# Attention inputs of a fused kernel loaded as one packed array, with a new order of work

## The chip, the cores and the metric

The kernel runs on one core of a Trainium2 chip. The metric is device time of one execution in microseconds (us), lower is better. A core has a matmul engine (PE, with its weight loads shown apart as PEld), three engines for elementwise work (DVE, ACT, POOL), and SP, which here only issues DMA loads and stores. Each engine takes its own instructions strictly in order. They wait for each other through semaphores.

## The reference

Sliding-window attention, then a mixture of experts with soft slots, then a gated feed-forward layer. All is f32.

```python
def _attn_ref(q, k, v):                      # 4 batches, 8 heads, 576 tokens, 64 wide
    scores = scale * np.matmul(q, k.transpose(0, 1, 3, 2))
    # heads 0-3: the last 32 tokens; heads 4-7: every 4th of the last 128
    scores = np.where(masks[None, :, :, :], scores, -1000000000.0)
    scores = scores - np.max(scores, axis=-1, keepdims=True)
    attn = np.exp(scores)
    attn = attn / (np.sum(attn, axis=-1, keepdims=True) + 1e-09)
    return np.matmul(attn, v).astype(np.float32)

def _moe_ref(x, phi, w1, w2):                # x: 2304 x 512
    logits = x @ phi                         # 8 experts x 4 slots
    d = softmax of logits over tokens;  slot_input = d.T @ x
    slot_out[e] = np.maximum(slot_input[e] @ w1[e], 0.0) @ w2[e]
    c = softmax of logits over slots;   return c @ slot_out

def _moe2_ref(x, w_in, w_out):               # 512 -> 2048 -> 512
    h = x @ w_in
    g = h * (1.0 / (1.0 + np.exp(-h)))
    return g @ w_out
```

## The kernel before

**Stages.** Two heads of one batch make a pair; there are 16 pairs. Stage one (0 to 97.4 us in the profile) is attention over the pairs together with the softmaxes of the slots, a batch after every fourth pair. Stage two (97.4 to 129.1 us) passes the slots through the experts: 16 pieces of w1 (operations `L1.0` to `L1.15`), then 16 of w2 (`L2.0` to `L2.15`, the last in two halves). Stage three folds the slots' output into w_in, and then runs the feed-forward layer over 6 groups of 384 tokens until the end. Its 864 large matmuls (`om`) are the bulk of the time: of each unit of hidden values, `si` (ACT, line 794) makes the plain value, `gh` (ACT at first, line 799) a rounded one and `gl` (DVE) the rest. Stage three can't begin before the last piece of w2 has been multiplied.

**One pair n, by the names of the operations.** `lq`, `lk`, `lv` load q, k and v, 288 KB each, 2304 bytes a partition (lines 165 to 184). `qx`, `qy` spread q into a padded place (POOL, line 180). `vx`, `vy` write a masked copy of v (line 197 on POOL, 199 on ACT, 201 on DVE). `M` and `S` put mask and scores into PSUM (PE, 36 matmuls for `S`). `rm` is the row maximum (DVE, 227), `ex` nine exponentials (ACT, 232), `rc` the reciprocal sums (DVE, 244), `nm` the normalization (POOL, 249), `pt` four transposes (DVE, 256 to 263). `pv` multiplies with v (PE, in two parts, `.0` and `.1`), `xe` copies the result out of PSUM (ACT, 299 or 301), `T` transposes it (PE, line 312), `te` copies that (ACT, 315), `lt` makes the logits (PE). For each batch `da`, `dt`, `dm`, `db`, `dq`, `dr`, `dsub`, `dex`, `dc` carry the softmax over tokens, and `caa` to `cag` the one over slots.

**What sets the order.** `op(name, engine, cost, deps, fn)` records each operation. `list_schedule` (line 1049) then plans all of them: it places an operation on its engine when its inputs are ready by the planner's own costs, and where several are ready the one with the longest path to the end plus a bonus by kind from the table `PRIO` goes first. The program is emitted in that order, so the table decides what stands behind what on every engine. The loads are chained by hand instead: the string `ATT` (line 1022) gives the order of SP's queue, `q` for the next pair's q and k, `v` for the next v, `w` for the next piece of w1 or w2. SP issues in that order, and a load whose place is still in use holds back all loads behind it.

**Places.** k, q and v have separate rings: k five places, then three, q four, v four, then two (`kslot`, `qslot`, `rslot`, lines 110 to 117), spread over the buffers `k`, `raw`, `more0` and `more1`. `more0` and `more1` become w15 and w16 when attention is done with them.

Of the kernel before, what the change touches and what calls it, by code (L numbers as in the profile page):

```python
# [32 lines left out]
def fused_kernel(ctx: ExitStack, tc: tile.TileContext, a: dict):  # L33
# [12 lines left out]
    dm = hsb[0:1, 352:352 + 5 * NS]  # L46
# [32 lines left out]
    def reg(key, off, n):  # L79
        return tiles[key][:, off:off + n]  # L80
# [25 lines left out]
    for place, key in (("ra", "a0"), ("rb", "a1"), ("rk", "k"), ("rv", "v"), ("rs", "raw"), ("rt", "px"), ("x", "xb"), ("w15", "more0"), ("w16", "more1")):  # L106
        new(place, key)


    def kslot(n):  # L110
        return n % 5 if n < 10 else (n - 10) % 3

    def qslot(n):
        return n % 4

    def rslot(n):
        return n % 4 if n < 12 else n % 2

    def before(slot, n):
        return max((m for m in range(n) if slot(m) == slot(n)), default=None)  # L120

    def kreg(n):
        i = kslot(n)
        return reg("k", 608 * i, 608) if i < 3 else reg(f"more{i - 3}", 1152, 608)

    def qraw(n):
        i = qslot(n)
        return reg("raw", 576 * i, 576) if i < 2 else reg("more0", 576 * (i - 2), 576)

    def vraw(n):  # L130
        if n == NPAIR - 1:
            return vz
        i = rslot(n)
        return reg("raw", 1152 + 576 * i, 576) if i < 2 else reg("more1", 576 * (i - 2), 576)

# [46 lines left out]
    def load_v(n):  # L182
        b, p = divmod(n, 4)
        sp.dma_start(out=vraw(n), in_=a["v"][b, p])

# [3 lines left out]
    def veng(n):  # L189
        return VY[n % 4] if n > 1 else "DVE"  # L190
# [141 lines left out]
    for n in range(NPAIR):  # L332
        b, p = divmod(n, 4)
        kb, rb = before(kslot, n), before(rslot, n)
        qb, vb = before(qslot, n), rb if n < NPAIR - 1 else None
        op(f"lk{n}", "SP", .74, [f"S{kb}"] if kb is not None else [], lambda n=n: load_k(n))
        op(f"lq{n}", "SP", .74, [f"qx{qb}", f"qy{qb}"] if qb is not None else [], lambda n=n: load_q(n))
        op(f"lv{n}", "SP", .74, [f"vx{vb}", f"vy{vb}"] if vb is not None else [], lambda n=n: load_v(n))
        for z in range(2):
            op(f"q{'xy'[z]}{n}", "DVE" if z and n not in QP else "POOL", .7, [f"lq{n}", f"S{n-2}" if n >= 2 else None], lambda n=n, z=z: spread(n, z))  # L340
        for z in range(2):
            op(f"v{'xy'[z]}{n}", veng(n) if z else "POOL", {"POOL": 1.4, "ACT": .68, "DVE": .745}[veng(n) if z else "POOL"], [f"lv{n}", f"pv{n-2}.1" if n >= 2 else "izm", ("nm0", "rc0")[z] if n == 1 else None], lambda n=n, z=z: vmask(n, z))
# [3 lines left out]
        op(f"S{n}", "PE", 1.11, [f"M{n}" if n else "fl0", f"lk{n}", f"qx{n}", f"qy{n}", f"iq{n}" if n < 5 else None] + [f"iz{c}{n}" for c in "ab" if n < 2] + free,  # L346
           lambda n=n: scores(n))
# [215 lines left out]
    att_r = [f"{c}{n}" for c in ("qx", "qy") for n in (N1 - 3, N1 - 2)] + [f"{c}{n}" for c in ("vx", "vy") for n in (N1 - 2, N1 - 1)]  # L563
    att_v = [f"pv{N1}.1", f"S{N1}"]
    free2 = {"rs": att_r, "ra": [f"pv{N1-1}.1", f"S{N1-1}"], "rk": [f"S{N1}"], "rb": att_v, "rv": att_v, "rt": att_v + [f"T{N1}", f"lt{N1}"],
             "w15": ["qx14", "qy14", "qx15", "qy15", "S8"], "w16": ["vx10", "vy10", "vx11", "vy11", "S9"]}
    for i in range(16):
# [345 lines left out]

    for n in range(5):
        op(f"iq{n}", "DVE", .1, [], lambda n=n: iq(n))
# [245 lines left out]
def lay(inputs):  # L1161
# [12 lines left out]
    out = {}  # L1174
    out["q"] = np.ascontiguousarray(heads(inputs["q"]).transpose(0, 1, 2, 4, 3)).reshape(B, 4, 128, S)
    out["k"] = np.ascontiguousarray(heads(inputs["k"]).transpose(0, 1, 2, 4, 3)).reshape(B, 4, 128, S)
    v = heads(inputs["v"]).reshape(B, 4, 2, NJ, 2, 32, D)
    out["v"] = np.ascontiguousarray(v.transpose(0, 1, 4, 2, 5, 3, 6)).reshape(B, 4, 128, NJ * D)
    row = np.arange(128)
# [38 lines left out]
```

## Time and profile before

| what | us |
|---|---|
| median of 3 runs | 360.08 (359.61 to 360.41) |
| the profiled execution | 360.57 |
| span from its first to its last instruction | 358.4 |
| PE busy in stage one, 0 to 97.4 | 90.81 |
| PE busy in stage two, 97.4 to 129.1 | 31.68 of 31.70 |
| PE busy in stage three, 129.1 to 358.4 | 224.17 of 229.30 |

The span is what the trace covers; the rest of the execution's 360.57 us lies around it. "Busy" is the time in which an engine has at least one instruction under way; where it is not busy, the trace names what ended the wait. Rates are given in GB/s of all loads together.

### The profile page before, as it was taken

What the parts mean: (1) busy time and instruction counts of PE and PEld (TensorE: products, weight loads), DVE (VectorE), ACT (ScalarE), POOL (GpSimd) and SP (SyncE); (2) the same over time, 40 slices, a digit from 0 to 9 for tenths busy, and PEclk for the clock granted to TensorE, in tenths of its full rate; (3) what the DMA queues carried; (4) which work ended last, traced back from release to release, by engine and by line L of the source; (5) the groups of instructions that cost most, each with busy time, mean ns of one, the idle gap of its engine ahead of it and who ended that gap; (6) DMA issues with size and microseconds to landing.
All of it is one profiled execution on the core that took longest, in us unless ns stands there. A gap on an engine that the chain in (4) does not pass through costs nothing.

```text
span 358.4 us, 7976 instructions
## 1 busy us (share of the span) xinstructions
PE 346.7 (97%) x3118; PEld 263.2 (73%) x3118; DVE 236.9 (66%) x547; ACT 165.1 (46%) x558; POOL 74.5 (21%) x121
## 2 busy tenths in 40 slices
PE   7999999998999989999999999999999999999995
PEld 3686877776533347877888888787888888888884
DVE  5877778699620589999999764585444744474445
ACT  3698989786240146594433342546522222222220
POOL 6988978565420000000000000000000000000000
PEclk9999999999999999999999999999999999999999
DMA  7999999999999999462630000000000400040004
GB/s 255 404 408 404 406 396 409 405 417 414 419 400 422 408 423 416 165 234 92 261 117 0 2 0 0 3 0 3 0 0 2 176 0 2 0 176 2 0 0 176
DMA packets 17460, 70.02 MB, mean 195 GB/s; under 512 B 1936, under 2 KB 2448, under 8 KB 11664
## 3 DMA queue, kind: packets, MB, share of 16 engines
q1 hardware_dynamic: 17424, 69.53, 49.2%
q8 instruction: 24, 0.39, 0.4%
q14 instruction: 12, 0.10, 0.1%
HBM read 64.80 MB, written 4.72 MB: 194 GB/s over the span
## 4 chain that ended last, share of the span: by engine, by line
PE 90%; ACT 3%; DVE 2%; POOL 1%; issue 1%; DMA 1%; DVEq 0%; ACTq 0%; POOLq 0%
PE ps L86 86%; PE ps L312 3%; ACT rt_px L232 1%; DMA rs_raw<-in_q 1%; PE ps L434 1%; POOL rv_v L907 1%; ACT rv_astk L711 1%; ACT rt_px L301 1%; ACT rt_gtm L794 0%; POOL rb_a L180 0%; ACT x_gz L799 0%; POOL ra_a L180 0%; DVE stats L227 0%; ACT x_xb L315 0%; DVE spaced L244 0%
## 5 line engine op out<-in xcount | busy, mean ns | idle before, releaser
L86 PE MATMUL ps<-w_ws,x_gz 128*128 128x512 f32 x432 | 107.3, 392 | 0.0
L794 ACT ACTIVATE rt_gtm<-ps 128x384 f32<-128x384 f32 x96 | 47.0, 492 | 113.2 <-PE ps L86 111.0
L86 PEld LDWEIGHTS ps<-w_ws,x_gz 128*128 128x128 f32 x432 | 80.2, 188 | 16.8 <-DVE x_gz L804 0.4
L86 PE MATMUL ps<-w_ws,w_gy 128*128 128x512 f32 (+1 forms) x219 | 53.7, 389 | 0.0
L232 ACT ACTIVATE rt_px<-ps,spaced 128x64 f32<-128x64 f32 x144 | 43.5, 332 | 10.3 <-DVE spaced L228 8.7
L801 DVE CAST x_gz<-rt_gtm 128x384 fp32r<-128x384 f32 x52 | 18.6, 358 | 42.8 <-ACT rt_gtm L794 42.7
L86 PEld LDWEIGHTS ps<-w_ws,w_gy 128*128 128x128 f32 x219 | 40.4, 188 | 8.3 <-issue 0.2
L804 DVE TENSOR_TENSOR x_gz<-rt_gtm,x_gz 128x384 fp32r<-128x384 f32 x64 | 35.6, 557 | 4.0
L232 ACT ACTIVATION_READ_ACCUMULATOR rt_px<-ps,spaced 128x1 f32 x144 | 32.4, 225 | 0.0
L86 PE MATMUL ps<-ct_ct,rv_astk 128*128 128x384 f32 x96 | 31.8, 338 | 0.3 <-ACT rv_astk L711 0.2
L801 DVE CAST w_gy<-rt_gtm 128x384 fp32r<-128x384 f32 x28 | 10.0, 357 | 20.8 <-ACT rt_gtm L794 20.8
L86 PEld LDWEIGHTS ps<-ct_ct,rv_astk 128*128 128x128 f32 x96 | 18.0, 188 | 5.0 <-ACT rv_astk L711 0.6
L249 POOL TENSOR_TENSOR rt_px<-rt_px,stats 128x576 f32<-128x576 f32 (+2 forms) x17 | 18.6, 1094 | 8.6 <-DVE stats L245 2.9
L804 DVE TENSOR_TENSOR w_gy<-rt_gtm,w_gy 128x384 fp32r<-128x384 f32 x32 | 17.8, 558 | 2.2
L86 PE MATMUL ps<-rk_ws,x_gz 128*128 128x512 f32 x72 | 18.2, 395 | 0.5 <-ACT x_gz L799 0.5
L86 PE MATMUL ps<-rb_ws,x_gz 128*128 128x512 f32 x72 | 17.9, 392 | 0.0
L86 PEld LDWEIGHTS ps<-rk_ws,x_gz 128*128 128x128 f32 x72 | 13.3, 188 | 3.5 <-ACT x_gz L799 0.8
L86 PEld LDWEIGHTS ps<-ra_a,rv_v 128*64 128x64 f32 x320 | 13.3, 137 | 3.2 <-issue 1.4
L86 PE MATMUL ps<-ra_a,rv_v 128*64 128x96 f32 (+2 forms) x320 | 15.1, 241 | 0.6 <-issue 0.3
L86 PEld LDWEIGHTS ps<-rb_ws,x_gz 128*128 128x128 f32 x72 | 13.4, 188 | 2.7
L86 PE MATMUL ps<-rb_a,rv_v 128*64 128x96 f32 (+2 forms) x320 | 14.5, 241 | 0.0
L86 PEld LDWEIGHTS ps<-rb_a,rv_v 128*64 128x64 f32 x320 | 13.1, 137 | 1.9 <-issue 0.9
(224 smaller groups left out, 513.2 us busy)
## 6 DMA issues: line engine op xcount, KB each, us to landing
w_wi<-in_w_in SPq DMA_DIRECT2D x7, 1024.0 KB, 11.4
w_wo<-in_w_out SPq DMA_DIRECT2D x5, 1024.0 KB, 6.9
rk_k<-in_k SPq DMA_DIRECT2D x12, 288.0 KB, 7.6
rs_raw<-in_v SPq DMA_DIRECT2D x9, 288.0 KB, 9.1
rs_raw<-in_q SPq DMA_DIRECT2D x8, 288.0 KB, 6.8
w_more<-in_q SPq DMA_DIRECT2D x8, 288.0 KB, 9.4
out<-w_ost SPq DMA_DIRECT2D x9, 256.0 KB, 2.2
rs_wo<-in_w_out SPq DMA_DIRECT2D x2, 1024.0 KB, 9.3
```

The source lines that it names most:

```text
L86: pe.matmul(out, lhsT=lhsT, rhs=rhs, start=start, stop=stop, skip_group_check=True)
L232: act.activation(out=preg(n)[:, j, :], in_=sj(n, j), func=ACTF.Exp, scale=D ** -0.5, bias=nmx[:, r, j // 3, j % 3:j % 3 + 1], accum_out=su ...
L249: pool.tensor_tensor(out=p, in0=p, in1=rinv[:, n % 2, j0:j1].rearrange("p (j o) -> p j o", o=1).to_broadcast([128, j1 - j0, 64]), op=ALU.mult)
L301: act.copy(out=x, in_=src)
L312: pe.transpose(ps[0:m, c:c + 128], x[:, 128 * t:128 * t + m], ident)
L434: pe.transpose(cbank(b, k)[:, c:c + m], cc[0:m, t].rearrange("p r s -> p (r s)"), ident[0:m, 0:m])
L711: act.copy(out=asl(f)[32 * r:32 * r + 32], in_=(aqh if r < 2 else aql)[rows])
L794: act.activation(out=gtm(u), in_=hb(u), func=ACTF.Silu)
L801: dve.tensor_copy(ghalf(u, 0), gtm(u))
L804: dve.tensor_tensor(out=ghalf(u, 1), in0=gtm(u), in1=ghalf(u, 0), op=ALU.subtract)
L907: pool.memset(vreg(n)[i:i + 32, :, int(i % 64 == 0), :], 0.0)
```

## The change

q and k of a pair, and v of the pair two before it, lie side by side in one array `kqv` in memory: 6912 bytes a partition. One load, again named `lq`, brings all three into one of four places of 1760 columns (three places from the 13th load on). A place is free when the scores of the pair that used it are done, and the masked copies of the v in it. The first load stays split (q, then k), the second has no v, and the last two v are loaded alone as `lv14` and `lv15`. v of pair n thus arrives with q and k of pair n + 2, and `vx`, `vy` wait for that load. There are 92 DMA instructions in place of 121; the bytes are the same. `ATT` is a new string, and every entry of `PRIO` has a new value (for example `S` -1.43 to -23.06, `T` 1.39 to 3.23, `vx` 1 to 10), so the planner puts out another order on every engine.

```diff
-    def load_k(n):
-        b, p = divmod(n, 4)
-        sp.dma_start(out=kreg(n)[:, 32:608], in_=a["k"][b, p])
-
-    def load_q(n):
-        b, p = divmod(n, 4)
-        sp.dma_start(out=qraw(n), in_=a["q"][b, p])
+    def load(m, c0, c1):
+        sp.dma_start(out=slot(m)[:, 32 + c0:32 + c1], in_=a["kqv"][m, :, c0:c1])
...
+    def place(m):
+        return m % 4 if m < 12 else (m - 12) % 3
+
+    def slot(m):
+        return reg(("raw", "raw1", "more0", "more1")[place(m)], 0, 1760)
 
     def kreg(n):
-        i = kslot(n)
-        return reg("k", 608 * i, 608) if i < 3 else reg(f"more{i - 3}", 1152, 608)
+        return slot(n)[:, 0:608]
 
     def qraw(n):
-        i = qslot(n)
-        return reg("raw", 576 * i, 576) if i < 2 else reg("more0", 576 * (i - 2), 576)
+        return slot(n)[:, 608:1184]
 
     def vraw(n):
-        if n == NPAIR - 1:
-            return vz
-        i = rslot(n)
-        return reg("raw", 1152 + 576 * i, 576) if i < 2 else reg("more1", 576 * (i - 2), 576)
+        return vz if n == NPAIR - 1 else slot(n + 2)[:, 1184:1760]
...
-        op(f"lk{n}", "SP", .74, [f"S{kb}"] if kb is not None else [], lambda n=n: load_k(n))
-        op(f"lq{n}", "SP", .74, [f"qx{qb}", f"qy{qb}"] if qb is not None else [], lambda n=n: load_q(n))
-        op(f"lv{n}", "SP", .74, [f"vx{vb}", f"vy{vb}"] if vb is not None else [], lambda n=n: load_v(n))
+        def used(m):
+            m = max((i for i in range(m) if place(i) == place(m)), default=-1)
+            return ([f"S{m}"] if m >= 0 else []) + ([f"vx{m-2}", f"vy{m-2}"] if m > 1 else [])
+
+        if n == 0:
+            op("lq0", "SP", .74, [], lambda: load(0, 576, 1152))
+            op("lk0", "SP", .74, [], lambda: load(0, 0, 576))
+        else:
+            op(f"lq{n}", "SP", 1.4 if n < 2 else 2.1, used(n), lambda n=n: load(n, 0, 1728 if n > 1 else 1152))
+        if n >= NPAIR - 2:
+            op(f"lv{n}", "SP", .74, used(n + 2) if n < NPAIR - 1 else [], lambda n=n: load_v(n))
...
-ATT = "qqvqwvwwqvqwvvwqvvqwqwvqvqwvvqwwvqwwwqvwwwvwwwwwwwwwwwwwwooiwwwii"
+ATT = "wqqqqwwqqwqwqwwwqqwqqwqwwwqwvwwwvwwwwwwwwwwwoowwiwiiw"
...
```

**SP at the start of the program**, first before, then after the change. `in_q`, `in_k`, `in_v`, `in_kqv` are the arrays loaded from; `in_w` is a piece of w1, `in_mask` and `in_ip` are constants.

```order
L171 DMA rs_raw<-in_q 128x576
L167 DMA rk_k<-in_k 128x576
L943 DMA ip<-in_ip 128x256
L184 DMA rs_raw<-in_v 128x576
L171 DMA w_more_115<-in_q 128x576
L167 DMA rk_k<-in_k 128x576
L184 DMA rs_raw<-in_v 128x576
L171 DMA w_more_115<-in_q 128x576
L167 DMA w_more_115<-in_k 128x576
```

```order
L155 DMA rk_raw_110<-in_kqv 128x1152
L931 DMA ip<-in_ip 128x256
L155 DMA w_more_115<-in_kqv 128x1728
L519 DMA ct_w1.0_185<-in_w 128x2048
L155 DMA w_more_116<-in_kqv 128x1728
```

The rows begin at pair 1. v of pair 0 stood in front of q and k of pair 2; now it arrives with them. v of pair 1 and q and k of pair 3, the last three rows before, are the last row now, and the first piece of w1 has moved in front of them.

**POOL a little later**, before and after. The copies into `ra_a` and `rb_a` are `qx`, `qy`, those into `rv_v` are `vx`, and `rt_px` is `nm`.

```order
L180 COPY rb_a_109<-rs_raw 64x18x32 x2
L197 COPY rv_v<-rs_raw 32x9x64 x2
L180 COPY ra_a_108<-w_more_115 64x18x32 x2
L249 ISA
L249 TENSOR_TENSOR rt_px<-rt_px,stats 128x576
L180 COPY rb_a_109<-w_more_115 64x18x32
L197 COPY rv_v<-rs_raw 32x9x64 x2
L249 TENSOR_TENSOR rt_px<-rt_px,stats 128x576
L180 COPY rb_a_109<-w_more_115 64x18x32
```

```order
L164 COPY rb_a_109<-rk_raw_110 64x18x32 x2
L898 MEMSET ones 32x1
L900 MEMSET x_xb 128x5 x5
L180 COPY rv_v<-w_more_115 32x9x64 x2
L164 COPY ra_a_108<-w_more_115 64x18x32 x2
L232 ISA
L232 TENSOR_TENSOR rt_px<-rt_px,stats 128x576
L180 COPY rv_v<-w_more_116 32x9x64 x2
L232 TENSOR_TENSOR rt_px<-rt_px,stats 128x576
L164 COPY rb_a_109<-w_more_116 64x18x32 x2
```

The order of `vx0`, `q` of pair 2 and `nm0` is kept; behind them, `vx1` and `nm1` now come ahead of both copies of pair 3's q, of which one stood in front of them.

**PE in the second half of attention**, around `T10` (line 312 before, 295 after). `x_xb,le` is `dc1`, `64x64 x18` are the scores `S13`, `64x64 x2` with `rv_v` is `pv10.1`, `rt_px,ip` is `lt`, `ones,hsb` is `dr1`.

```order
L86 MATMUL ps<-x_xb,le 32x129 x20
L86 MATMUL ps<-rk_k,rb_a_109 64x64 x18
L86 MATMUL ps<-ra_a_108,rv_v 64x64 x2
L86 MATMUL ps<-rt_px,ip 32x160 x2
L86 MATMUL ps<-rt_px,ip 32x128 x2
L86 MATMUL ps<-rt_px,ip 32x160 x2
L86 MATMUL ps<-rt_px,ip 32x128 x2
L86 MATMUL ps<-ones,hsb 128x1
L312 MATMUL ps<-ip,rt_px 128x128 x4
L312 MATMUL ps<-ip,rt_px 64x128
```

```order
L86 MATMUL ps<-ra_a_108,rv_v 64x64 x2
L86 MATMUL ps<-ones,hsb 128x1
L86 MATMUL ps<-rk_raw_110,rb_a_109 64x64 x18
L295 MATMUL ps<-ip,rt_px 128x128 x4
L295 MATMUL ps<-ip,rt_px 64x128
L86 MATMUL ps<-rt_px,ip 32x160 x2
L86 MATMUL ps<-rt_px,ip 32x128 x2
```

The scores of the pair three ahead now stand between the last part of `pv` and `T`, and `lt` directly behind `T`. So it is now for every pair from 0 to 12; before, it was not for `T7`, `T8`, `T10` and `T11`. Behind this place, `dt2` and `db2` stand in front of `pv13`, where they stood behind it, `dc2` in front of `T13`, where it stood behind, and `dr2` between `pv14.1` and `T14`. On ACT, where stage three begins, `gh` of the first two units (line 799, PE's first large matmuls read it) stands in front of their `si` (line 794), where each stood behind its own.

## Rows read from the trace of the kernel before

**Rows 1.** The page's second part: GB/s moved in 40 equal slices of the span.
```profile
GB/s 255 404 408 404 406 396 409 405 417 414 419 400 422 408 423 416 165 234 92 261 117 0 2 0 0 3 0 3 0 0 2 176 0 2 0 176 2 0 0 176
```

**Rows 2.** The chain that ended last: start us, us, what.
```profile
11.45 0.41 ACT rt_px L232 x2
11.91 6.86 PE ps L86 x125
...
133.00 0.49 ACT rt_gtm L794
133.49 0.39 ACT x_gz L799
...
169.06 185.50 PE ps L86 x882
```

**Rows 3.** Stretches: us, each engine's busy us (instructions), clock, DMA share, GB/s.
```profile
10.30:16.20 5.90, 5.68 (x69) 3.25 (x71) 4.87 (x12) 2.77 (x19) 5.37 (x7) 1.00 1.07 407
86.20:98.50 12.30, 11.35 (x160) 7.05 (x158) 8.68 (x34) 4.24 (x10) 5.40 (x9) 1.00 1.01 418
```

**Rows 4.** Timeline of SP: start us, us, the load of k for pair 2.
```profile
4.47 0.54 SPq L167 DMA_DIRECT2D rk_k<-in_k  x1
```

**Rows 5.** DMA issues between 4.45 and 4.50: KB, us from issue to landing.
```profile
rk_k<-in_k SPq DMA_DIRECT2D x1, 288.0 KB, 5.7
```

**Rows 6.** DMA issues between 113.4 and 113.5: the second half of w2.15.
```profile
w_w2.15_1819<-in_w SPq DMA_DIRECT2D x1, 512.0 KB, 13.9
```

**Rows 7.** Timeline of POOL at the start: start us, us, instruction, count, wait.
```profile
8.91 1.36 POOL L197 COPY rv_v<-rs_raw 32x576 f32<-32x576 f32 x2
10.22 1.38 POOL L180 COPY ra_a<-w_more 64x576 f32<-64x576 f32 x2
11.85 1.15 POOL L249 TENSOR_TENSOR rt_px<-rt_px,stats 128x576 f32<-128x576 f32 x1 [0.25 <-ACT rt_px L232]
...
13.76 1.36 POOL L197 COPY rv_v<-rs_raw 32x576 f32<-32x576 f32 x2
15.20 1.15 POOL L249 TENSOR_TENSOR rt_px<-rt_px,stats 128x576 f32<-128x576 f32 x1
```

**Rows 8.** Timeline of DVE at the start: `vy0` and `rm1`.
```profile
8.84 0.81 DVE L201 TENSOR_SCALAR rv_v<-rs_raw,zm 128x576 f32<-128x576 f32 x1 [1.40 <-DMA rs_raw<-in_v]
10.40 0.76 DVE L227 TENSOR_REDUCE stats<-ps 128x9 f32<-128x576 f32 x1 [0.75 <-ACT rt_px L232]
```

**Rows 9.** Timeline of PE: in brackets, idle us before and what ended it.
```profile
17.49 1.27 PE L86 MATMUL ps<-w_more,rb_a 128*64 128x64 f32 x36
...
31.75 0.81 PE L86 MATMUL ps<-rk_k,ra_a 128*64 128x64 f32 x21 [0.81 <-issue]
...
57.45 0.77 PE L312 MATMUL ps<-ip,rt_px 128*128 128x128 f32 x5 [0.33 <-ACT rt_px L299]
...
69.08 0.77 PE L312 MATMUL ps<-ip,rt_px 128*128 128x128 f32 x5 [0.25 <-ACT rt_px L301]
...
73.59 0.77 PE L312 MATMUL ps<-ip,rt_px 128*128 128x128 f32 x5 [0.37 <-ACT rt_px L301]
...
81.67 0.40 PE L86 MATMUL ps<-hsb,ones 1*128 1x32 f32 x2 [0.45 <-DVE hsb L381]
...
85.09 1.72 PE L86 MATMUL ps<-ra_a,rv_v 128*64 128x96 f32 x40 [0.25 <-DVE ra_a L263]
87.61 0.76 PE L312 MATMUL ps<-ip,rt_px 128*128 128x128 f32 x5 [0.79 <-ACT rt_px L301]
...
128.10 1.04 PE L86 MATMUL ps<-w_w2.15_1819,x_sip 128*32 128x512 f32 x8
...
133.92 1.66 PE L86 MATMUL ps<-rk_ws,x_gz 128*128 128x512 f32 x6 [0.50 <-ACT x_gz L799]
```

**Rows 10.** DMA queues between 0 and 97.4: packets, MB, share of 16 engines.
```profile
q8 instruction: 13, 0.21, 0.9%
```

**Rows 11.** DMA queues between 29.0 and 30.2, the same columns.
```profile
q8 instruction: 1, 0.02, 5.4%
```

More of the change, by code (lines that the diff above doesn't have):

```diff
@@ L103, in op @@
         ops[name] = (eng, cost, [d for d in deps if d], fn)
-    for place, key in (("ra", "a0"), ("rb", "a1"), ("rk", "k"), ("rv", "v"), ("rs", "raw"), ("rt", "px"), ("x", "xb"), ("w15", "more0"), ("w16", "more1")):
+    for place, key in (("ra", "a0"), ("rb", "a1"), ("rk", "raw1"), ("rv", "v"), ("rs", "raw"), ("rt", "px"), ("x", "xb"), ("w15", "more0"), ("w16", "more1")):
         new(place, key)
[L110 to L120, printed above, removed]
+    def place(m):
+        return m % 4 if m < 12 else (m - 12) % 3
+    def slot(m):
+        return reg(("raw", "raw1", "more0", "more1")[place(m)], 0, 1760)
     def kreg(n):
-        i = kslot(n)
-        return reg("k", 608 * i, 608) if i < 3 else reg(f"more{i - 3}", 1152, 608)
+        return slot(n)[:, 0:608]
     def qraw(n):
-        i = qslot(n)
-        return reg("raw", 576 * i, 576) if i < 2 else reg("more0", 576 * (i - 2), 576)
+        return slot(n)[:, 608:1184]
     def vraw(n):
-        if n == NPAIR - 1:
-            return vz
-        i = rslot(n)
-        return reg("raw", 1152 + 576 * i, 576) if i < 2 else reg("more1", 576 * (i - 2), 576)
+        return vz if n == NPAIR - 1 else slot(n + 2)[:, 1184:1760]
     def qreg(n):
@@ L182, in load_v @@
     def load_v(n):
-        b, p = divmod(n, 4)
-        sp.dma_start(out=vraw(n), in_=a["v"][b, p])
+        sp.dma_start(out=vraw(n), in_=a["kqv"][n + 2 - NPAIR, :, 1152:1728])
     def vact(n):
@@ L341, in fused_kernel @@
         for z in range(2):
-            op(f"v{'xy'[z]}{n}", veng(n) if z else "POOL", {"POOL": 1.4, "ACT": .68, "DVE": .745}[veng(n) if z else "POOL"], [f"lv{n}", f"pv{n-2}.1" if n >= 2 else "izm", ("nm0", "rc0")[z] if n == 1 else None], lambda n=n, z=z: vmask(n, z))
+            op(f"v{'xy'[z]}{n}", veng(n) if z else "POOL", {"POOL": 1.4, "ACT": .68, "DVE": .745}[veng(n) if z else "POOL"], [f"lq{n+2}" if n < NPAIR - 2 else f"lv{n}", f"pv{n-2}.1" if n >= 2 else "izm", ("nm0", "rc0")[z] if n == 1 else None], lambda n=n, z=z: vmask(n, z))
         free = [exn(n - 2) if n >= 2 else None, ex1(n - 1) if n else None]
@@ L345, in fused_kernel @@
             op(f"M{n}", "PE", .3, ["cmask", f"fl{n}" if n in FILL and n < 3 else None, f"S{n-1}"] + free, lambda n=n: masks(n, True))
-        op(f"S{n}", "PE", 1.11, [f"M{n}" if n else "fl0", f"lk{n}", f"qx{n}", f"qy{n}", f"iq{n}" if n < 5 else None] + [f"iz{c}{n}" for c in "ab" if n < 2] + free,
+        op(f"S{n}", "PE", 1.11, [f"M{n}" if n else "fl0", f"lq{n}" if n else "lk0", f"qx{n}", f"qy{n}", f"iq{n}" if n < 4 else None] + [f"iz{c}{n}" for c in "ab" if n < 2] + free,
            lambda n=n: scores(n))
@@ L562, in fused_kernel @@
     N1 = NPAIR - 1
[L563 removed]
     att_v = [f"pv{N1}.1", f"S{N1}"]
[L565 to L566 removed]
+    free2 = {"rs": [f"S{N1}", f"vx{N1-2}", f"vy{N1-2}"], "ra": [f"pv{N1-1}.1", f"S{N1-1}"], "rk": [f"S{N1-2}", f"vx{N1-1}", f"vy{N1-1}"], "rb": att_v, "rv": att_v, "rt": att_v + [f"T{N1}", f"lt{N1}"],
+             "w15": [f"S{N1-1}", f"vx{N1-3}", f"vy{N1-3}"], "w16": ["S11", "vx9", "vy9"]}
     for i in range(16):
@@ L912, in ix @@
             pool.memset(xreg(i)[:, :, 128:129], 1.0)
-    for n in range(5):
+    for n in range(4):
         op(f"iq{n}", "DVE", .1, [], lambda n=n: iq(n))
@@ L955, in fused_kernel @@
     ol = ["lwo0", "lwo1"]
-    loads = ["lq0", "lk0", "cmask", "lq1", "lk1", "cip", "lv0", "lq2", "lk2", "lv1"]
-    vs = [f"lv{n}" for n in range(2, NPAIR)]
+    loads = ["lq0", "lk0", "cmask", "lq1", "cip", "lq2"]
+    vs = [f"lv{n}" for n in range(NPAIR - 2, NPAIR)]
     n = 3
@@ L960, in fused_kernel @@
         if c == "q":
-            loads += [f"lq{n}", f"lk{n}"]
+            loads.append(f"lq{n}")
             n += 1
@@ L1174, in lay @@
     out = {}
[L1175 to L1178, printed above, removed]
+    q, k = (heads(inputs[n]).transpose(0, 1, 2, 4, 3).reshape(NPAIR, 128, S) for n in "qk")
+    v = heads(inputs["v"]).reshape(B, 4, 2, NJ, 2, 32, D).transpose(0, 1, 4, 2, 5, 3, 6).reshape(NPAIR, 128, NJ * D)
+    out["kqv"] = np.ascontiguousarray(np.concatenate([k, q, np.roll(v, 2, 0)], 2))
     row = np.arange(128)
```

5 lines of the change are left out of this document (2 added, 3 removed).

## The prediction

> **What bounds the kernel now.** I read the slices of the page first. The loads move some 400 to 420 GB/s from the second slice to the sixteenth [rows 1], so the queue never runs dry before the last of w2 is in; a change that moves no bytes less can only gain by their order and by the rate. Then the chain. From 11.91 us on it is almost all PE, and 185.50 us at the end are one piece of matmuls, the same before and after [rows 2]. The 31.68 busy of 31.70 us in stage two leave nothing there. So a gain can come only from PE's waits in stage one and at the seam to stage three, and a loss from new waits in the same places. These I took from PE's timeline [rows 9].
>
> **The sum's own base.** The profiled execution took 360.57 us, the median of the runs is 0.49 lower. I add the terms to the first and then take off the 0.49.
>
> **Fewer, longer loads.** 14 loads of 885 KB (decimal) replace 42 of 295 KB. Bytes of 2304 a partition moved at 407 GB/s, bytes of 8192 a partition at 418 [rows 3]. 885 KB take 2.17 us at the one rate and 2.12 at the other, so the whole stream gets shorter by nothing to 14 x 0.057 = 0.8 us. As 6912 is near 8192, I take 0.7. The Trainium skill speaks for much more ("DMA: Bandwidth & Descriptors", section on bandwidth: batch to 1 MiB or more for 75% of peak, with a fixed part of about 2 us a DMA). By that, as an estimate, two fixed parts less in each of 14 loads would be 56 us; the rows do not agree, since loads queued behind each other move 97% (407 of 418) of what the long ones do, so the fixed part is hidden already. The 29 issues less on SP are worth nothing: its issues lie under transfers under way.
>
> **The start: a loss.** k of pair 2 is issued at 4.47 and lands 5.7 later, at 10.2 [rows 4, 5]. The same bytes stand in front of the end of the changed kernel's third load, so this one lands at about 10.1, and v of pair 0 with it. DVE began `vy0` at 8.84, having waited for that load, and POOL `vx0` at 8.91 [rows 7, 8]. Both now wait until 10.1, and everything behind them on their engines with them. On DVE `rm1` moves from 10.40 to 10.1 + 0.8 = 10.9, on the chain. On POOL I go on: `vx0` 1.36, the copies of pair 2's q 1.38 and `nm0` 1.15 end at 14.0, not 13.0. Next stands `vx1`, whose v comes with load 3, and in front of load 3 is now the first piece of w1: 10.1 + 1.05 MB at 418 (2.5) + 2.1 = 14.7. `vx1` ends at 16.1, `nm1` at 17.2 and the copies of pair 3's q at 18.6. `S3`, which started at 17.49 [rows 9], needs them: +1.1. PE has no idle time in the next 13 us in which to win that back. Bounds: 0.5 if only `rm1` counts, 1.9 if the piece of w1 takes 0.8 longer.
>
> **Attention's second half: a gain.** Three times `T` waited for `xe` on ACT, at 57.45, 69.08 and 73.59, for 0.33, 0.25 and 0.37 [rows 9]. These are `T8`, `T10` and `T11`, the ones in front of which `S` did not stand. 36 matmuls of 1.27 now fill that time, more than `xe` and its signals took. I take all 0.95; the end on the other side is 0, if ACT, which has little to spare there, just comes later.
>
> **The last pairs: a gain.** `db2` waited 0.45 for `dm2` on DVE, `pv14` 0.25 for its transposes, `T14` 0.79 for `xe14` [rows 9], at 81.67, 85.09 and 87.61. `dt2` and `db2` now run a pair earlier, the transposes of pair 14 are no longer broken up by work of pair 15 and of the slots, and `dr2` (0.31 with what lies around it) fills a part of the third. 0.45 + 0.25 + 0.3 = 1.0, bounds 0 and 1.49. What is late next is `pv15`: its reciprocals now stand behind five DVE operations of the slots.
>
> **The cap.** Together -0.95 - 1.0 + 1.1 = -0.85 when w1 begins. Stage two then hits the loads. The last half of w2.15, issued at 113.46, lands 13.9 later, at 127.35 [rows 6]; PE's matmuls on w2.15 begin at 128.10 [rows 9], and those on this half 0.43 behind, at 128.5. In the new queue two quarters of w_in (0.52 MB, 1.25 us) stand in front of it: 127.35 + 1.25 - 0.7 = 127.9, or 128.6 without the faster rate. Of 0.85 at most 0.6 gets through.
>
> **The seam: a gain.** PE waited 0.50 for the first `gh`, since ACT did `si` (0.49) ahead of it; both are on the chain [rows 2, 9]. With `gh` first that goes: -0.5, bounds 0 and 0.5. The second `ah` on ACT, now behind four of these, is needed some 2 us later and just makes it.
>
> **Sum.** -0.6 - 0.5 = -1.1. I take 0.2 off for waits that a new order makes and that no row shows: -0.9, so 360.57 - 0.9 = 359.7 for an execution like the profiled one, and **359.2** for the median.
>
> **Rival 1, only the loss stays: slower.** Its place is load 3 behind the piece of w1, its price 1.1, as above. If each wait that the order removes comes back under another name (PE, ACT and POOL are all busy in stage one, so `T` may find ACT behind again), stage one keeps all of it, and w1 begins 1.1 later: 361.2. For it: the delay is worked out from arrivals, the gains only from the order. Against: the three waits of `T` fall on just the places that the order changes. It decides the sign as soon as less than 0.2 to 0.4 of the 1.95 is won.
>
> **Rival 2, the loads cap it.** If longer rows move no faster, the last half of w2 lands at 128.6, PE waits for it, and whatever stage one wins is lost; only the seam stays, less the new waits: 359.8 to 360.1, no change that can be told. What can be told of this kernel is about 0.2%, 0.72 us.
>
> **Rival 3, late instructions: slower.** In stage one PE's instructions come in 13 blocks of 16 KB on a queue of their own [rows 10]. One block lands between 29.0 and 30.2 [rows 11], and at 31.75 PE goes on after 0.81 without a semaphore to wait for [rows 9], in the middle of `S6`. So a block can come late while data loads fill the engines. If a block must wait for the load's share in progress on its engine, that share grows from 0.72 to 2.17 us for a third of the stage's bytes: half of 1.45 more, in a third of the cases, 13 times, is 3.1 us, and 362.3 in all. Against: one such stall of this size in 13 blocks, while pieces of w1, longer still, were two thirds of the traffic. The Trainium skill has the rule for it ("DMA: Bandwidth & Descriptors", queues, rings and completion order: an engine drains a whole packet, typically 9 to 17 descriptors, of one ring before it turns to another); the rows above fit it, but do not show that the wait grows with the row's length.
>
> **Rival 4, the change does not do what it says.** If places came free too late, SP would hold back all loads behind one and the stream would have holes. A place is used again by the fourth pair after, some 18 us later at 4.4 us a pair, and a load is issued 8 to 14 us ahead of its landing, so I see none.
>
> **Chances.** The forecast 0.40, from 358.5 (all bounds good: 0.6 + 0.5 and the stream 0.4 faster) to 359.5. Rival 2 and things between 0.32. Rival 1 0.18. Rival 3 0.08. Rival 4 0.02. Range 358.3 to 361.6: it leaves out rival 3 and 4 and some of each end. Faster by over 0.2% 0.40, within 0.34, slower 0.26.
>
> **What would show it.** The first wait of DVE on the third load ending near 10.1, `vx1` waiting on POOL until about 14.7, and `S3` at 18.6. No waits of `T` for ACT over 0.2 between 50 and 75. w1 begins at 96.6, not 97.4. The last half of w2.15 landing near 127.9, PE reaching it at the same time. No wait of 0.5 in front of the first large matmuls. I am wrong if `S3` is not late, if w1 begins after 98, or if PE shows more stalls like the one at 31.75.

## The result and the profile after

The changed kernel is slower: 363.45 us (median of 13 runs, 360.86 to 366.48) against 360.30 (13 runs, 359.61 to 360.75), ratio 1.0084, 95% interval 1.0061 to 1.0107. That is outside the range of the prediction, and on the other side of no change. The ratio leaves out a run that lies over 1.5% above the fastest of its kernel, here the one of 366.48. The profiled execution took only 361.31, less than most runs. The table shows when PE reaches a few points of the program, in that profile, in a second profile of the same kernel and in that of the best version found below:

| us | before | after | after, again | best version |
|---|---|---|---|---|
| `S3` begins | 17.49 | 19.47 | 19.62 | 18.30 |
| first matmul on w1 | 97.42 | 96.73 | 97.34 | 96.12 |
| first large matmul | 133.92 | 133.07 | 134.11 | 132.63 |
| the 101st large matmul (a hundred are done) | 161.97 | 162.82 | 165.46 | 160.67 |
| time of this execution | 360.57 | 361.31 | 363.94 | 358.87 |

From there on all four need the same 192.5 to 192.8 us to the end of the last large matmul. So the result is made before 166 us. The new order is ahead by 0.85 at the first large matmul, behind by the same 0.85 at the 101st (expectations below call it the hundredth), and in the second profile behind by 3.5.

The loads of the changed kernel, in the page's 40 slices (before: [rows 1]):

```profile
GB/s 259 424 412 383 418 416 416 419 411 419 406 395 416 403 425 419 223 118 96 256 117 0 2 0 0 3 0 2 1 0 2 175 0 2 0 176 2 0 0 175
```

The early slices are faster than before (424 and 412, not 404 and 408), but the fourth dips to 383. The start on POOL answers to [rows 7], and the wait of DVE to [rows 8]:

```profile
10.79 1.38 POOL L180 COPY rv_v<-w_more 32x576 f32<-32x576 f32 x2 [0.77 <-DMA w_more<-in_kqv]
12.11 1.38 POOL L164 COPY ra_a<-w_more 64x576 f32<-64x576 f32 x2
13.55 1.14 POOL L232 TENSOR_TENSOR rt_px<-rt_px,stats 128x576 f32<-128x576 f32 x1
15.38 1.37 POOL L180 COPY rv_v<-w_more 32x576 f32<-32x576 f32 x2 [0.69 <-DMA w_more<-in_kqv]
16.84 1.15 POOL L232 TENSOR_TENSOR rt_px<-rt_px,stats 128x576 f32<-128x576 f32 x1
18.06 1.36 POOL L164 COPY rb_a<-w_more 64x576 f32<-64x576 f32 x2
...
10.84 0.81 DVE L184 TENSOR_SCALAR rv_v<-w_more,zm 128x576 f32<-128x576 f32 x1 [2.54 <-DMA w_more<-in_kqv]
```

`vx0` waits for load 2 until 10.79, `vx1` for load 3 until 15.38, and the copies for `S3` end at 19.4. PE's timeline, answering to [rows 9]: the row of `S3`; the row on w2.15, which has no bracket; and, of the rows behind 25 us, all whose bracket shows a wait of more than 0.3:

```profile
19.47 1.27 PE L86 MATMUL ps<-w_more,rb_a 128*64 128x64 f32 x36 [0.26 <-POOL rb_a L164]
...
86.29 0.77 PE L295 MATMUL ps<-ip,rt_px 128*128 128x128 f32 x5 [0.49 <-ACT rt_px L284]
88.18 1.91 PE L86 MATMUL ps<-rb_a,rv_v 128*64 128x96 f32 x40 [0.73 <-DVE rb_a L246]
...
127.38 1.30 PE L86 MATMUL ps<-w_w2.15_1792,x_sip 128*32 128x512 f32 x8
129.16 1.08 PE L86 MATMUL ps<-s,x_sip 128*128 128x32 f32 x8 [0.47 <-ACT x_sip L577]
...
133.07 2.09 PE L86 MATMUL ps<-rk_ws,x_gz 128*128 128x512 f32 x8 [0.41 <-ACT x_gz L787]
...
155.09 0.50 PE L86 MATMUL ps<-w_ws,x_gz 128*128 128x512 f32 x1 [1.18 <-ACT w_ws L654]
155.96 1.42 PE L86 MATMUL ps<-w_ws,x_gz 128*128 128x512 f32 x5 [0.37 <-DVE w_ws L743]
```

The waits of `T` between 50 and 75 are gone, and so is the stall at 31.75 that waited for no semaphore. At 88.18 stands a new one, of `pv15` for its transposes. From `S3` to the first matmul on w1, before and then after (stretch, us, busy us of PE, PEld, DVE, ACT and POOL, clock, DMA share, GB/s):

```profile
17.49:97.42 79.93, 75.85 (x1504) 59.52 (x1503) 61.72 (x175) 64.28 (x295) 56.19 (x84) 1.00 1.02 408
19.47:96.73 77.26, 75.94 (x1504) 59.47 (x1504) 61.47 (x176) 63.76 (x293) 55.98 (x84) 1.00 1.01 411
```

PE is busy as long as before, and idle for 1.32 in place of 4.08. The eight matmuls on w2.15 take 1.30, not 1.04: the last half comes late, inside the row. And at 155 stands a wait that the kernel before does not have: 1.18 for `wh4` (the rounded weights of unit 4, line 654 on ACT), then 0.37 for `wl4`. Where it comes from is on ACT and DVE:

```profile
151.71 0.68 DVE L622 SCALAR_TENSOR_TENSOR w_wt<-rs_wo,w_wt 128x512 uint32<-128x512 uint32 x1
...
152.75 0.50 ACT L787 ACTIVATE x_gz<-ps 128x384 fp32r<-128x384 f32 x1
153.14 0.49 ACT L782 ACTIVATE rt_gtm<-ps 128x384 f32<-128x384 f32 x1
153.51 0.50 ACT L787 ACTIVATE x_gz<-ps 128x384 fp32r<-128x384 f32 x1
153.88 0.51 ACT L782 ACTIVATE rt_gtm<-ps 128x384 f32<-128x384 f32 x1
154.42 1.14 ACT L654 CAST w_ws<-w_wt 128x512 fp32r<-128x512 f32 x2
```

DVE ends `cvo4` (the unit's weights, which `wh4` reads) at 152.39, as early as before (152.33), but ACT now does `gh` and `si` of both halves of unit 4 ahead of `wh4`, which starts at 154.42. Before, `wh4` came first:

```profile
152.71 0.62 ACT L666 CAST w_ws<-w_wt 128x512 fp32r<-128x512 f32 x1
```

### The profile page after: what moved, and what is told of

Read it like the earlier page. It is cut to its first block, busy times and chain, and to the rows that moved or that the text cites. A ratio compares the mean times of both kernels' runs of the same rounds, so it can differ in the third digit from the quotient of the medians.

```text
span 359.5 us, 7932 instructions
## 1 busy us (share of the span) xinstructions
PE 347.9 (97%) x3118; PEld 263.2 (73%) x3118; DVE 236.0 (66%) x546; ACT 165.1 (46%) x558; POOL 74.5 (21%) x121
## 4 chain that ended last, share of the span: by engine, by line
PE 83%; DVE 6%; ACT 3%; DMA 3%; POOL 2%; issue 1%; SPq 1%; DVEq 0%; POOLq 0%; ACTq 0%
PE ps L86 79%; DMA w_more<-in_kqv 3%; PE ps L295 3%; ACT rt_px L215 1%; DVE x_gz L792 1%; PE ps L423 1%; DVE w_wt L620 1%; POOL rb_a L164 1%; DVE ra_wif L622 1%; DVE ra_wif L620 1%; POOL rt_px L232 1%; DVE w_wt L622 1%; DVE w_wt L618 0%; SPq L155 0%; ACT rt_gtm L782 0%
## 5 line engine op out<-in xcount | busy, mean ns | idle before, releaser
L86 PE MATMUL ps<-rb_a,rv_v 128*64 128x96 f32 (+2 forms) x320 | 15.1, 242 | 0.7 <-DVE rb_a L246 0.7
L86 PE MATMUL ps<-ra_a,rv_v 128*64 128x96 f32 (+2 forms) x320 | 14.7, 242 | 0.3 <-DVE ra_a L246 0.3
```

Of the source, the lines that this page charges most:

```text
L86: pe.matmul(out, lhsT=lhsT, rhs=rhs, start=start, stop=stop, skip_group_check=True)
```

## The experiments

All were run in five rounds against the kernel before; the 95% intervals reach 0.1 to 0.3% to either side. Names of operations in a diff stand for their place in the order of one engine.

**The same kernel again.** No edit.

> The changed kernel once more, nothing edited. Its profiled execution took 361.31, but the median of 13 is 363.45 and they reach from 360.86 to 366.48, where the kernel before spreads by 1.1 over 13. So some 2 us of the typical run are not in the first profile. Theory A (a wait that comes and goes, such as late instructions or late loads): the five runs spread over 2 us or more again, and a profile of a longer one shows waits of PE at block boundaries or for loads in stage one. Theory B (TensorE's clock): longer runs show a mean granted clock of 0.995 or less and a stretch at the low level.

363.68 (ratio 1.0079, 1.0059 to 1.0099). This profile took 363.94 and shows what the first one lacks. PE's rows at 155, then three stretches of the second profile. The columns are as above; the granted clock is TensorE's, as a share of the full 2.4 GHz:

```profile
156.18 0.50 PE L86 MATMUL ps<-w_ws,x_gz 128*128 128x512 f32 x1 [1.19 <-ACT w_ws L654]
157.06 2.13 PE L86 MATMUL ps<-w_ws,x_gz 128*128 128x512 f32 x5 [0.38 <-DVE w_ws L743]
159.00 0.52 PE L86 MATMUL ps<-ct_ct,rv_astk 128*128 128x384 f32 x1
159.32 2.96 PE L86 MATMUL ps<-w_ws,x_gz 128*128 128x512 f32 x9
```

```profile
155.00:157.00 2.00, 0.50 (x1) 0.19 (x1) 2.00 (x5) 1.94 (x6) 0.00 (x0) 1.00 0.63 209
157.00:161.00 4.00, 3.94 (x11) 3.15 (x12) 3.38 (x8) 3.50 (x10) 0.00 (x0) 0.57 0.37 158
161.00:164.00 3.00, 3.00 (x15) 2.50 (x14) 2.23 (x7) 2.13 (x6) 0.00 (x0) 1.00 0.00 0
```

The wait is the same. Behind it the granted clock is 0.57 over four microseconds: with two levels, 1.2 and 2.4 GHz, that is (1 - 0.57) / 0.5 x 4 = 3.4 us at the lower, in which half the work is done, so 1.7 us are lost. In the first profile the clock stayed at 1.00 behind the same wait. Of the 19 runs so far, 12 have a mean granted clock of 0.995 or less, which is one such spell (two at 0.991); of the kernel before, none. The median of these 12 is 363.68, that of the other seven 361.87. So theory B holds for a part, and 12/19 x 1.7 = 1.1 us is its mean share. Theory A has a part too: in the second profile w1 begins 0.6 later, and the row on w2.15 takes 1.73, since the last half of it lands at 128.6, not 127.6. And the seven runs without the low clock still reach from 360.86 to 366.19.

**The wait at unit 4, first try.** ACT and DVE:

```diff
-ah3 ... gh0.4.0 si0.4.0 gh0.4.1 si0.4.1 wh4
+wh4 gh0.4.0 si0.4.0 ah3 ... gh0.4.1 si0.4.1
-cvd5 cvo4 al3 cvo5 cvc6 gl0.4.0 cvd6 gl0.4.1 wl4
+cvo4 cvd5 gl0.4.0 al3 wl4 cvo5 cvc6 cvd6 gl0.4.1
```

> The changed kernel, with the conversion of the fifth piece of w_out moved: wh4, then gh and si of that unit, ahead of ah3 on ACT, and cvo4, wl4 earlier on DVE. PE waits 1.18 + 0.37 at 155 us in the profile of the changed kernel. Theory A (this wait is most of what the seam loses, and nothing later hides it): 1.3 to 1.6 faster than the changed kernel. Rival (PE is then held at the next unit by DVE, which is just as late): 0.5 or less faster. If the long idle of PE also sets off the low clock of some runs, the spread falls to about 1 us and the median by 2 or more beyond that.

362.41. In this kernel `gh` and `wh4` stood in the program ahead of what they read, so they did not wait for it and worked on older values. Nor did the wait go: it stands at 155.14 with 1.17, where a matmul of `h` waits for `si` of unit 4 (line 782 on ACT). So its time tells nothing of what the wait costs. It had no low clock in 6 runs.

**The start, first try.**

```diff
-ATT = "wqqqqww..."
+ATT = "qwqqqww..."
+        for c, d in ((1152, 1728), (0, 1152)) if m == 2 else ((c0, c1),):
```

> The changed kernel, with v of pair 0 in a load of its own ahead of the rest of the third load, and the load of pair 3 ahead of the first piece of w1. In the changed kernel S3 began at 19.47, 1.98 later than before. Theory A (the arrival of v0 and of pair 3 sets the start): vx0 near 9, S3 near 17.5, w1 begins 1.5 to 2 earlier, but the last half of w2, which lands at 127.6, lets only 0.3 to 0.5 of it through: 0.3 to 0.5 faster than the changed kernel. Rival (PE's instruction blocks pace stage one): S3 moves by 2 but w1 begins less than 0.7 earlier.

365.83, slower, against both. `ATT` also feeds the planner, which made another order of all engines: `S3` began at 18.15, but `pv` of pair 2 then waited 2.11, from 24.8 to 26.9, for its transposes on DVE, which stood behind `nm2` on POOL (to 24.69). (The expectation of the next try of the start names `nm3` there.) Behind that wait the clock fell too:

```profile
20.00:27.00 7.00, 4.89 (x104) 3.76 (x104) 3.96 (x13) 5.77 (x27) 6.58 (x10) 1.00 1.01 416
27.00:32.00 5.00, 5.00 (x82) 4.41 (x83) 3.23 (x8) 3.38 (x19) 2.54 (x8) 0.66 0.95 387
```

All later edits of loads or of the order keep the rest of the order word for word.

**Short rows.** Each packed load as three.

```diff
+        for c in range(c0, c1, 576):
+            sp.dma_start(out=slot(m)[:, 32 + c:32 + c + 576], in_=a["kqv"][m, :, c:c + 576])
```

> The changed kernel, with each packed load issued as three loads of 2304 bytes a partition, in the same place and order. Theory A (long rows delay the instruction fetch and cause the loss and the spread): 2 to 3 faster than the changed kernel, spread about 1. Theory B (row length matters only by the rate, 0.05 us a pair): same or up to 0.8 slower, the spread stays at several us.

364.44 (1.0116, 1.0092 to 1.0140): 0.8 slower than with long rows in the same rounds, with intervals that overlap. So the long rows are not the loss.

**The wait at unit 4, second try.** The places of the first try, with every operation named behind what it reads.

> The changed kernel with one edit in its order: on ACT wh4, then gh and si of the first half of unit 4, stand ahead of ah3; on DVE cvo4 ahead of cvd5, and wl4 ahead of cvo5. Every other instruction, and all loads, keep their order. Theory A (the loss is mainly the wait of PE at 155 us, 1.18 + 0.37, and the 3.4 us at the low clock that follow it in more than half of the runs, some 1.7 each): median 360.8 to 361.3 where the changed kernel has 363.7, no run with a mean clock of 0.995. Rival (the clock falls for another reason): 1.3 to 1.6 faster, and half of the runs keep 0.995.

361.98 (1.0056). The wait was not removed: `al3` waits for `ah3`, which now comes later, and `wl4` behind it came at 154.77. PE waited 1.65 and 0.45. Even so 6 of 6 runs had no low clock. 361.98 is level with the 361.87 of the changed kernel's runs without it, so all of the gain can be that alone.

**The start, order kept.** v of pair 0 ahead of the rest of its load, as in the first try, and on SP

```diff
-lq2 lw1.0 lq3
+lq2 lq3 lw1.0
```

> The changed kernel with two edits in its loads, and the order of every other engine kept word for word: v of pair 0 comes in a load of its own ahead of the rest of the third load, and the load of pair 3 stands ahead of the first piece of w1. (In the run before with these loads the planner had made a new order, in which pv waited 2.1 for nm3.) Theory A: vx0 near 9, S3 near 17.5 in place of 19.5, w1 begins 1.5 to 2 earlier, the last half of w2 holds PE for the rest, 0.2 to 0.6 faster than the changed kernel. Rival: POOL is the bound of the first pairs, S3 moves by less than 1 and nothing is left at the end.

361.43 (1.0038, 1.0017 to 1.0059), 2.0 less than the changed kernel. `S3` begins at 17.79, w1 at 95.15, and the loads have no dip any more:

```profile
GB/s 270 422 416 417 418 415 414 420 411 416 406 406 413 410 422 421 185 117 112 240 117 0 2 0 0 3 0 2 1 0 2 175 0 2 0 176 2 0 0 175
```

So the late start also held back the loads: the load of pair n + 4 waits for the scores of pair n. I had expected only 0.2 to 0.6; not foreseen was that the last half of w2.15 comes earlier as well, at 126.8. PE still waits for it: it reaches w2.15 at 125.81, and the row takes 2.07.

**The last half of w2.15 first.**

```diff
-... lw2.15 lwi0.1 lwi0.2 lw2b ...
+... lw2.15 lw2b lwi0.1 lwi0.2 ...
```

> The changed kernel with one edit: the last half of w2.15 is loaded ahead of the second and third piece of w_in, as before the change. The last eight matmuls on w2.15 took 1.30, 1.73 and 1.93 in three traces of this order, 1.04 before. Theory A (PE waits there for the load): the half lands 1.25 earlier, these matmuls take 1.04 again, 0.3 to 0.9 faster than the changed kernel. Rival (the pieces of w_in then come too late for the seam): no gain, a new wait in front of the first aqh.

361.54 (1.0040). The row on w2.15 is back at its length, though the half landed no earlier than in the first profile, since this run's start was late:

```profile
128.68 1.06 PE L86 MATMUL ps<-w_w2.15_1792,x_sip 128*32 128x512 f32 x8
```

Three single edits thus gave back 1.5 to 2.0 of 3.2 us each, more than each one's own mechanism explains. Common to them is that the low clock got rarer: 5 of 12 runs with the start, 1 of 8 with w2.15, and 0 of 6 at unit 4. These counts are small, and 5 of 12 is not clear of 12 of 19.

**The packed loads alone.** Two tries: PE, ACT, DVE and POOL in the order of the kernel before, SP with packed loads.

> The packed loads alone: PE, ACT, DVE and POOL keep the order of the kernel before, and SP loads packed q, k, v where it loaded q and k, nothing where it loaded v, the rest as before. Theory A (the new order is what loses at 155 us and at w2.15; the layout only costs at the start): 360 to 361.3, no low clock, spread below 2. Rival (the packed loads, with four places, make the loss by holding back the stream): 362 or more, slices of the loads under 390 GB/s between 25 and 45.

365.94. Level up to the 101st large matmul (161.85), but the engines' programs had been interleaved another way, and PE got four waits that have nothing to do with the loads, the first of them

```profile
227.61 1.08 PE L86 MATMUL ps<-w_wif,lg 128*32 128x128 f32 x32 [0.58 <-ACT rt_gtm L782]
```

This matmul writes the last 128 columns of a bank of PSUM (the memory that PE writes to), whose first 384 ACT's `si` reads (lines 674 and 784 of the kernel before). In the kernel before it starts at 227.07 and that `si` behind it, at 228.23; here the program names `si` first, and the matmul waits. So the interleaving matters beside the order of each engine. With it kept:

> The packed loads alone again: the whole emission order of the kernel before, the interleaving of the engines too, which the earlier try had changed (there PE got new waits of 0.58 to 0.90 between 227 and 258 us that have nothing to do with the loads; up to 162 us it was level with the kernel before, 161.85 against 161.97). Theory A (the layout costs nothing in the old order): 360.0 to 360.8. Rival (the layout costs 1 or more by itself, at the start): 361.3 or more.

360.23 against 360.15 of the kernel before in the same rounds: 1.0003 (0.9994 to 1.0013). The packed loads cost nothing and give nothing in time. The stream is faster at first (slices 2 to 7 of the 40 move 410 to 422 GB/s, before 396 to 409) and slower later (slices 10 to 12 move 391, 391 and 358, before 414, 419 and 400). All of the loss is in the order, that of the loads included.

**Unit 4, mended.** As in the second try, but on DVE

```diff
-cvo4 cvd5 gl0.4.0 al3 wl4 cvo5 cvc6
+cvo4 cvd5 wl4 cvo5 gl0.4.0 al3 cvc6
```

> The order edit again, mended: in the run before, al3 on DVE stood ahead of wl4 and waited for ah3, so PE's wait at 155 us became 1.65 + 0.45 and was not removed; all the same no run showed a mean clock of 0.995. Now wl4, cvo5 and gl of unit 4 stand ahead of al3. Theory A (this wait costs its full length, and the low clock comes with it at some places only): PE's waits between 150 and 160 fall from 1.55 to under 0.4, no run under 0.997, median 360.2 to 361.2. Rival (DVE and ACT are full there, the wait comes back at the next unit): 361.5 or more.

361.49 (1.0062). No wait for `wh4` or `wl4` is left; a smaller one took its place, for the copies on ACT that `h` of unit 5 reads, and one of 11 runs has the low clock. Against the kernel before it is no better than the second try (1.0062 and 1.0056), and nearest to the rival's 361.5:

```profile
153.63 1.80 PE L86 MATMUL ps<-w_ws,x_gz 128*128 128x512 f32 x6
156.28 0.45 PE L86 MATMUL ps<-ct_ct,rv_astk 128*128 128x384 f32 x1 [0.84 <-ACT rv_astk L699]
```

**All three.** The start, w2.15 and unit 4 as last mended.

> The changed kernel with the three edits together: v of pair 0 first and the load of pair 3 ahead of the first piece of w1; the last half of w2.15 ahead of two pieces of w_in; the order of unit 4 as in the run beside it. Theory A (three separate losses that add: start about 1.5 to 2, w2.15 about 0.5 once the start is early, the wait at 155 about 1.5): 358.2 to 359.4, faster than the kernel before by 1 to 2. Rival (each gain is eaten by the next limit): 360 or more.

360.99 (1.0025, 1.0014 to 1.0036), no low clock in 12. The rival was right: the gains do not add. PE has new waits, 0.74 at the seam (at 131.34) and 0.86 at unit 4 (at 155.68).

**Load 3 alone.** SP's edit of the start, without that of v.

> The changed kernel with one edit: the load of pair 3 ahead of the first piece of w1; v of pair 0 stays in the third load. Both edits together gained 2.0 in the median. If each half counts by its own delay (vx0 1.9 late, vx1 1.6 late against before), this one alone gains 0.8 to 1.4: 362.1 to 362.8. If only the order of load 3 counts: 361.4. If only v0 counts: 363.5.

361.15 (1.0035). `S3` at 18.60, w1 at 95.36, one low clock in 12. That is 2.3 of 3.2, nearest to the 361.4 expected if only the order of load 3 counts: v of pair 0 in a load of its own added nothing here (361.43 with both). The low clock is rare here too.

**Matmuls that keep PE busy.** Nothing moved.

```diff
+            if name == "om0.0.4":
+                for _ in range(8):
+                    mm(bank[6][:, 0:128], ident, ident, True, True)
```

> The changed kernel with nothing moved: eight matmuls of 128 x 128 on a constant, whose result nobody reads, stand in front of the first matmuls of unit 4, where PE waits 1.18 at 155 us. They take about 1.2. Theory A (the idle of PE there brings the low clock of 12 in 19 runs, and that is most of what the median has above the first profile): no run with a mean clock of 0.995, median 361.3 to 361.9. Rival (the low clock has another cause): about half of the runs at 0.995, median 363 to 364.

362.49 (1.0051). PE is busy through the wait, and 0 of 8 runs have the low clock, where 12 of 19 had it:

```profile
155.43 2.01 PE L86 MATMUL ps<-ip 128*128 128x128 f32 x16
157.20 1.90 PE L86 MATMUL ps<-w_ws,x_gz 128*128 128x512 f32 x6
```

So PE's idle time there brings the low clock in this kernel: 363.68 - 362.49 = 1.2 of the median. 362.49 - 360.30 = 2.2 are left over the kernel before; this profile has a late start (w1 at 98.28).

**The order cut in two at the last matmul of w2.** Old order, then new:

> The opposite: packed loads and the old order up to the last matmul of w2 (which alone ran level with the kernel before), the new order from there on. Theory A (the new order of the third stage loses by itself): the seam gains 0.4, the waits at unit 4 cost 1.55, some runs have the low clock: 361.2 to 362.5. Rival (the loss comes only from the first two stages): 360.5 or less.

362.34 (1.0055, 1.0038 to 1.0073): the new order of stage three loses 2.1 by itself (362.34 for 360.29 of the kernel before and 360.23 of the packed loads alone). It has the wait at 155 (1.19 and 0.37) and the low clock in 2 of 6 runs. New order and new loads, then old order:

> The new order and the new queue of loads, unchanged, up to the last matmul of w2, and the old order from there on: the fourth corner of a square, whose others are old and old (packed loads alone, 360.23), old and new (362.34), new and new (363.6). Theory A (the loads' order costs what the new order of the first stages gains, about 1): 360.2 to 361.0. If the two halves simply added: 361.4. Rival (the gain of the faster version came from the order, not from the two moved loads): 359.5.

360.49 (1.0000, 0.9984 to 1.0016): the new order of the first two stages is level, no low clock in 12. The halves do not add up: 2.1 for stage three and 0.1 for the first two are less than the 3.2 of both. About 0.5 of the rest is the low clock, by an estimate from the counts (12 of 19 runs and 2 of 6, 1.7 each); what makes the other half is open. With load 3 and the last half of w2.15 moved ahead:

> The new order up to the last matmul of w2, with two loads moved (pair 3 ahead of the first piece of w1, the last half of w2.15 ahead of two pieces of w_in); from there on the order of the kernel before on PE, ACT and DVE. Theory A (the new order gains in the first two stages, once its loads are right, and loses in the third): w1 begins near 95.4, the first large matmul near 132.5, the hundredth near 160.5 where the kernel before has 161.97: 358.6 to 359.3. Rival (DVE's conversions of the weights, not PE, pace the third stage's start, whatever the order): 360 or more.

359.44 (0.9978, 0.9966 to 0.9990): faster than both kernels. And with v of pair 0 in a load of its own too:

> The faster version (new order up to the last matmul of w2, load of pair 3 ahead of the first piece of w1, last half of w2.15 ahead of two pieces of w_in, old order from there on) and v of pair 0 in a load of its own ahead of the rest of the third load. Theory A (v0 arrives 1.5 earlier, PE's first two waits shrink by 0.6, and nothing stands between them and w2.15 now): 0.2 to 0.6 faster than the version without it (359.44): 358.8 to 359.2. Rival (POOL and ACT are full behind it): the same.

358.42 (0.9949, 0.9933 to 0.9965), 2.0 faster than the kernel before in the same rounds (360.38), and 5.0 than the changed one. The stream comes early enough for w2.15, and unit 4 waits no more than before:

```profile
18.30 1.27 PE L86 MATMUL ps<-w_more,rb_a 128*64 128x64 f32 x36
...
126.78 1.07 PE L86 MATMUL ps<-w_w2.15_1793,x_sip 128*32 128x512 f32 x8
128.34 1.08 PE L86 MATMUL ps<-s,x_sip 128*128 128x32 f32 x8 [0.49 <-ACT x_sip L578]
132.63 1.66 PE L86 MATMUL ps<-rk_ws,x_gz 128*128 128x512 f32 x6 [0.51 <-ACT x_gz L788]
153.47 0.44 PE L86 MATMUL ps<-ct_ct,rv_astk 128*128 128x384 f32 x1 [0.26 <-ACT rv_astk L700]
```

## Why the prediction was wrong

**The step that failed: "I take 0.2 off for waits that a new order makes and that no row shows".** In the profiled execution the new waits at 155 are 1.55, and with what follows the kernel falls from 0.85 ahead to 0.85 behind within 30 us. For all of stage three the sum had -0.5 for the seam and +0.2 for new waits; its new order alone measured +2.1 (k_stage3), low clock included. I followed ACT's new order through the first two units of stage three and costed the rest at nothing. The new order held the warning: PE had no time to give there, ACT's `wh` of each unit is on the way to PE, and `wh4` had moved behind four operations, which took from 152.75 to 154.39. At the start I had gone on along POOL's queue behind the moved `vx`; I did not do the same on ACT at unit 4.

**The base.** The median was put 0.49 below the profiled execution, as before the change. It lies 2.1 above, and two things make the runs differ. One is the low clock, 1.1 in the mean. The other is stage one: in the eight profiles with this order and these loads up to w1 (the two above, e1_w4_early, f1_w4_early, f3_w2b_first, h_w4, j_fill and l_new12), w1 begins between 95.70 and 98.28. It begins latest, at 97.97 to 98.28, in the three whose fourth slice of the loads moves least (333 to 348 GB/s; the others 383 to 392). That the hole in the loads makes w1 late fits, but was not tried apart. The 12 runs of l_new12 have no low clock and differ by 3.0. None of the 8 runs with matmuls in that wait has the low clock, nor any of the 12 with the packed loads alone, 12 with all three edits, 12 each of the first two versions with the old order behind w2, and 6 of the last.

**The start** was late, as forecast, but by 2.0, not 1.1. The loads came 0.7 later than worked out (`vx0` 10.79 for 10.1, `vx1` 15.38 for 14.7); the other 0.2 lies between the operations on POOL that follow. Its second effect, on the loads behind, was rival 4's ("If places came free too late") and was given 0.02; with the edits of the start it vanishes.

**Attention's second half and the last pairs.** w1 began at 96.73 where 96.6 was forecast, but that is luck: the start lost 0.9 more than forecast, and PE's idle time behind it shrank by 2.8, not 1.95. The waits of `T` went, as forecast (0.95). With them went stalls of PE without a semaphore to wait for, on which the sum had not counted: 0.81 at 31.75, and the other 0.5 between 50 and 75, where PE's idle time fell from 1.48 to nothing. The last pairs gave 0.5, not 1.0 (1.78 to 1.32 idle behind 75): the wait of `pv15`, 0.73, is the one that the prediction called late next and put no price on.

**The cap** was right in its place: landing 127.6 for 127.9, and PE waits 0.26. In the ten other profiles with this half behind two pieces of w_in the row takes 1.20 to 2.22.

**The seam** gained 0.38 of the 0.5: `sotm`, the first matmul behind w2, began 0.47 earlier than before (129.16 for 129.63), the first large matmul 0.85 earlier.

**Fewer, longer loads** moved more GB/s, as forecast, but the packed loads alone gained no time (1.0003).

**Rival 1** (361.2) has the right sign for a wrong reason: it let the start's loss alone stay, but the first two stages are level (l_new12). **Rival 2**, no change that can be told, is true of the first two stages, but not of the end. **Rival 3** gave the nearest number, 362.3, and did not happen: PE has no stall of that kind over 0.3 between 25 and 85 us, and short rows were no faster.

**Still open** is why the same wait brings the low clock in 12 of 19 runs of the changed kernel, but in 1 of 12 with load 3 moved and in 5 of 12 with v0 as well; why the two halves together lose 1 us more than the sum of each alone; and why v of pair 0 by itself gives 1.0 in the best version and nothing in the changed kernel. And what the first stages' order would give with the loads' order planned for it was not tried further.

## What to carry to other kernels

When a table moves every instruction, follow each engine's queue through the whole stretch in which PE has no slack, not only through the places that had waits before: a wait that goes is seen in the trace, a wait that comes is not. Try the parts of such a change apart, in a square of old and new halves; here one half was level, one lost, and the first with two or three loads moved gave the gain that was meant. When a total comes out as forecast, check its terms: w1 came on time because two errors cancelled. And look at the spread: a kernel whose 13 runs differ by 5.6 us where they differed by 1.1 has something that comes and goes, and a second profile is cheaper than a theory.

## What the runs showed of the hardware

- Behind two waits of PE (1.19 and 0.38, one matmul between them) the granted clock was at 1.2 GHz for 3.4 us in one profile (e0_again), and behind two of 1.18 and 0.37 it stayed at 2.4 GHz in another. Eight small matmuls in the idle time kept it up in 8 of 8 runs (j_fill).
- With the packed loads of 6912 bytes a partition among the pieces of w1, the stream moved 410 to 422 GB/s in slices 2 to 7 (g2_layout); with loads of 2304 bytes in their place, 396 to 409 in the kernel before. No time was gained by it.
- A load lands when the last of its parts does, and instruction blocks share the engines. From issue to landing load 3 took 12.2 us in the profile of the first try at unit 4 (e1_w4_early) and 11.3 in the changed kernel's (same loads, same order). In the first, an instruction block is under way in the last 3 us of that load, 13.2 to 16.2; in the second there is none. The issue and the queues of the first:

```profile
w_more<-in_kqv SPq DMA_DIRECT2D x1, 864.0 KB, 12.2
```

```profile
q8 instruction: 1, 0.02, 2.2%
```

  That fits a delay of 0.9 by the block; it was not tried apart.
- The Trainium skill says that a DMA's semaphore reaches its full count only when every engine's share of the data has landed ("DMA: Bandwidth & Descriptors", section on why a DMA increments its semaphore by 16). The trace agrees: of that load, 15 shares came in between 13.6 and 15.1 and the last at 16.2, and `vx1` started at 16.23, behind it.
